# An attention and feed-forward kernel on one core: its opening replanned with a shared-port rule, paired scores and prescaled queries, and written in fixed order until chunk 3's x is turned

## The chip, the cores and the metric

The kernel runs on one core of one Trainium2 chip. The metric is device time in microseconds (us) of one execution, and the time of a kernel is the median of its runs. The engines are named as in the profile: PE is TensorE's matmul stream (PEld its weight loads), DVE is VectorE, ACT is ScalarE, POOL is GpSimd, SP is SyncE, which here only issues DMA transfers. "L1388" is line 1388 of the kernel.

## The reference

`q`, `k` and `v` have the shape batch 8, heads 8, sequence 576, head width 64. Two attentions are added: a coarse one over means of four tokens, and a local one over tokens less than four apart. The sum, laid out as 4608 tokens of width 512, is normalised and goes through a gated feed-forward layer with 1536 inner columns.

```python
q_d = q.reshape(B, H, Sd, 4, D).mean(axis=3)          # k_d, v_d likewise; Sd = 144
out_up = np.repeat(sm_attn(q_d, k_d, v_d), 4, axis=2)  # softmax attention, scale 1/8
mask = np.abs(pos[:, None] - pos[None, :]) < 4
scores = np.where(mask, scale * q @ k.T, -1e9)         # then softmax, then @ v
attn_out = out_up + out_local
x = attn_out.transpose(0, 2, 1, 3).reshape(B * S, H * D)
xn = x / np.sqrt(np.mean(x * x, -1) + 1e-6) * rms_g
g = xn @ w_gate
out = (g / (1 + np.exp(-g)) * (xn @ w_val)) @ w_out
```

## The kernel before

The tokens are worked through in 18 chunks of 256. A chunk has two stages. The first makes its `x`, normalises it and turns it, so that the 512 columns lie on partitions. The second (`Forward`) is the feed-forward layer: for each of six pairs n of 128-column blocks, `first` computes gate and value products into `ps_h` (L1388), ACT and DVE make the gated product from them (`tanh`, `gate` L1399, `product` L1404, `high` L1410, `low` L1413), and `second` multiplies it with the output weights into `ps_o` (L1427). Every f32 operand is split into a high and a low part and three products are added, so a pair takes 48 + 12 matmuls, and all 18 chunks take 5184 of L1388 and 1296 of L1427. Once chunks overlap, the feed-forward of one chunk runs on PE while DVE, ACT and POOL make the `x` of a later one.

There are two ways to make `x`. Chunks 2 to 17 use `Attention`: products of q and windows of k and v on DVE (L917, L921, L970, L980), with help from ACT and POOL. The first two chunks use `Early`, which is shorter and goes through PE. For each of a chunk's two units and each of four head pairs n, `score` puts a mask matmul (L1166, against `near_sb`) and the q times k matmuls (L1168) into a `ps_h` tile. DVE's `peak` finds the row maximum (L1181), `less` scales it (L1185), ACT's `powers` takes exponentials (L1192), DVE's `invert` makes the reciprocal of the sum (L1198, L1199), `edges` and `shares` multiply by it (L1211, L1219), PE turns the result (L1227, L1238), a copy brings it back to SBUF (L703 on ACT, L705 on DVE), and `value` (L1258) and `spread` (L1265) give a unit's rows in PSUM. `spread` adds the coarse attention of batch 0. Copy, squares, `rms`, three Newton steps (`root`, L729 to L731), `norm`, the turn of x (L1303) and its split into `xh` and `xl` (L1306, L1310) follow, and then the chunk's first L1388 can run.

The coarse attention (`Coarse`, per batch and head pair) is scores L593, maximum L603, its scaling L608, exponentials L613, reciprocal L644 and L647, turn L623, copies, values L638 and scaling L656. For batch 0 its sums over four tokens are made from loaded raw data, which `Early` also reads (L473 for q and k, L481 for v). For the other batches they are summed by DMAs that add.

All weights are decoded in the opening. They lie in HBM as 64-bit words; a piece is fetched by SP (L309), ACT scales it (L315), POOL extracts three last bits (L325), DVE joins them (L332), ACT makes the high part (L339, for gate and value multiplied by `g_sb`, the norm's gain) and DVE the low part (L346, L344).

The order of all this up to chunk 2's feed-forward and chunk 3's `x` is set by a planner in the kernel (`Plan`). A task has an engine (or a choice of two), a cost, a due time, predecessors and buffers. The planner goes forward in its own time: of an engine's ready tasks that could start within `NEAR` of the earliest, the one with the lowest number in the table `RANK` is next; DMA transfers are put one after another at `MB` us per MB. Within `tc.manual_schedule()` instructions are emitted in this order, until planned time `due[FIRST] + 10` (224 us); the rest of the planned tasks, and chunks 3 to 17 that follow in loops, are ordered by the framework's scheduler. An engine works its queue strictly in order.

Where the planner sees PE idle, `heat` (L504) puts in 512-column (or 256-column) bf16 matmuls into an unused tile, so that PE keeps its clock. Until the first `value` of `Early` that needs it, one of the two `ps_o` tiles is spare and takes them.

POOL's queue holds small loads (`load_edges` L1147, queries L906, `load_small` L1532 to L1536 with `min_sb`, `g_sb` and `same_sb`), `make_one` (`one_sb`, L1500), parts of L1151, L481, L970 and L1413, all of L325, and the adding DMAs (L417).

Of the kernel before, what the change touches and what calls it, by code (L numbers as in the profile page):

```python
# [1654 lines left out]
```

## Time and profile before

| | |
|---|---|
| median of 3 runs | 1091.54 us (1090.29 to 1092.67) |
| the profiled execution | 1089.94 us, of it 1088.1 us span of instructions |
| PE busy | 1066.7 us (98%), 7983 matmuls |
| DVE busy | 909.6 us (84%) |
| ACT busy | 598.6 us (55%) |
| POOL busy | 160.8 us (15%) |
| granted PE clock, mean | 0.992 |

The page gives busy times per engine, and the span in 40 slices of 27 us with a digit in tenths for each engine. A view of windows gives the same for chosen stretches, with the granted clock; a timeline lists instructions with their start and duration, and in brackets how long the engine stood idle before, and what ended that. A view of groups adds up the instructions of one line and shape: the count, total busy time, mean in ns of one, and idle time of the engine just before them. Busy PE includes `heat`, and a matmul's duration overlaps the next, so PE's share is not useful work.

### The profile page before, as it was taken

What the parts mean: (1) busy time and instruction counts of PE and PEld (TensorE: products, weight loads), DVE (VectorE), ACT (ScalarE), POOL (GpSimd) and SP (SyncE); (2) the same over time, 40 slices, a digit from 0 to 9 for tenths busy, and PEclk for the clock granted to TensorE, in tenths of its full rate; (3) what the DMA queues carried; (4) which work ended last, traced back from release to release, by engine and by line L of the source; (5) the groups of instructions that cost most, each with busy time, mean ns of one, the idle gap of its engine ahead of it and who ended that gap; (6) DMA issues with size and microseconds to landing.
All of it is one profiled execution on the core that took longest, in us unless ns stands there. A gap on an engine that the chain in (4) does not pass through costs nothing.

```text
span 1088.1 us, 21642 instructions
## 1 busy us (share of the span) xinstructions
PE 1066.7 (98%) x7983; PEld 970.2 (89%) x7983; DVE 909.6 (84%) x1554; ACT 598.6 (55%) x2029; POOL 160.8 (15%) x200
## 2 busy tenths in 40 slices
PE   7899999999999999999999999999999999999997
PEld 4569899899989999999999999999999999999996
DVE  7799999798969897979797979798998898986421
ACT  4686565737266565656564737383737373645111
POOL 6544564300210101010101010100000000000000
PEclk9899999999999999999999999999999999999999
DMA  9885657333654535353525253522221222210000
GB/s 292 274 237 167 182 134 155 77 91 86 132 102 117 118 99 102 107 106 87 126 85 128 68 130 86 132 77 82 63 86 54 79 78 74 80 40 20 1 20 20
DMA packets 79182, 114.09 MB, mean 105 GB/s; under 512 B 33038, under 2 KB 40406, under 8 KB 79076
## 3 DMA queue, kind: packets, MB, share of 16 engines
q1 hardware_dynamic: 48308, 88.40, 26.3%
q0 software_dynamic: 11680, 19.78, 11.6%
q10 hardware_dynamic: 19088, 4.53, 1.9%
q8 instruction: 62, 1.02, 0.4%
q14 instruction: 44, 0.36, 0.1%
HBM read 100.86 MB, written 11.80 MB: 104 GB/s over the span
## 4 chain that ended last, share of the span: by engine, by line
PE 85%; DVE 6%; DMA 3%; issue 2%; POOL 2%; ACT 1%; SPq 1%; DVEq 0%; POOLq 0%; ACTq 0%
PE ps_h L1388 51%; PE ps_o L1427 25%; PE ps_a L638 3%; DMA w<-in_w_val_dram 1%; PE ps_a L593 1%; PE ps_a L623 1%; DVE prod L917 1%; PE ps_a L1033 1%; DVE x_t L980 1%; DVE sc L921 1%; PE ps_a L1258 1%; DVE sil L1404 0%; POOL hs L1413 0%; DMA vs<-in_v_sum_dram 0%; DMA wo<-in_w_val_dram 0%
## 5 line engine op out<-in xcount | busy, mean ns | idle before, releaser
L1388 PE MATMUL ps_h<-xh,w 128*128 128x256 f32 x3456 | 632.6, 281 | 0.0
L1388 PEld LDWEIGHTS ps_h<-xh,w 128*128 128x128 f32 x3456 | 537.6, 188 | 9.7 <-issue 3.1
L1388 PE MATMUL ps_h<-xl,w 128*128 128x256 f32 x1728 | 482.5, 280 | 0.0
L1427 PE MATMUL ps_o<-wo,hs 128*128 128x512 f32 x1296 | 327.1, 396 | 4.2 <-POOL hs L1413 1.7
L1388 PEld LDWEIGHTS ps_h<-xl,w 128*128 128x128 f32 x1728 | 325.2, 188 | 5.8 <-issue 2.0
L963 ACT ACTIVATE prod<-kv,sc 128x64 f32<-128x64 f32 x1024 | 261.9, 406 | 28.9 <-DVE sc L954 15.5
L1427 PEld LDWEIGHTS ps_o<-wo,hs 128*128 128x128 f32 x1296 | 232.8, 188 | 49.1 <-DVE hs L1413 2.8
L980 DVE TENSOR_REDUCE x_t<-prod 128x128 f32<-128x896 f32 x128 | 134.5, 1080 | 39.5 <-PE ps_a L1033 36.8
L1410 ACT ACTIVATE hs<-sil 128x512 fp32r<-128x512 f32 x108 | 68.2, 631 | 165.5 <-DVE sil L1404 140.1
L1396 ACT ACTIVATE sil<-ps_h 128x512 f32<-128x512 f32 x108 | 64.1, 595 | 148.7 <-PE ps_h L1388 140.8
L917 DVE TENSOR_TENSOR prod<-q_t,kv 128x896 f32<-128x896 f32 x128 | 138.6, 1089 | 0.2
L921 DVE TENSOR_REDUCE sc<-prod 128x14 f32<-128x896 f32 x128 | 136.9, 1075 | 0.2
L1399 DVE SCALAR_TENSOR_TENSOR sil<-sil,ps_h 128x512 f32<-128x512 f32 x108 | 73.7, 683 | 52.1 <-ACT sil L1396 52.1
L970 DVE TENSOR_TENSOR prod<-sc,kv 128x384 f32<-128x384 f32 (+1 forms) x128 | 105.9, 868 | 0.1
L1404 DVE SCALAR_TENSOR_TENSOR sil<-sil,ps_h 128x512 f32<-128x512 f32 x108 | 73.9, 684 | 22.6 <-PE ps_h L1388 22.1
L417 POOL DMA_DIRECT2D qk<-in_qk_sum_dram x42 | 39.0, 928 | 340.0 <-DMA qk<-in_qk_sum_dram 282.1
L1413 DVE TENSOR_TENSOR hs<-sil,hs 128x512 fp32r<-128x512 f32 x102 | 69.9, 685 | 17.9 <-ACT hs L1410 17.8
L613 ACT ACTIVATE a_g<-ps_a,m_g 72x144 f32<-72x144 f32 x128 | 46.5, 370 | 54.2 <-DVE m_g L608 50.0
L417 POOL DMA_DIRECT2D vs<-in_v_sum_dram x42 | 39.4, 937 | 104.1 <-DMA vs<-in_v_sum_dram 80.7
L1003 ACT ACTIVATE up_t<-x_t 128x128 f32<-128x128 f32 x128 | 39.1, 305 | 18.3 <-DVE x_t L993 12.2
L638 PEld LDWEIGHTS ps_a<-vs,a_g 72*72 72x72 f32 x512 | 39.2, 150 | 7.4 <-ACT a_g L613 2.9
L638 PE MATMUL ps_a<-vs,a_g 72*72 72x64 f32 x512 | 40.8, 234 | 5.1 <-ACT a_g L613 2.7
(154 smaller groups left out, 808.0 us busy)
## 6 DMA issues: line engine op xcount, KB each, us to landing
kv<-in_k_pad_dram SPq DMA_DIRECT2D x56, 320.0 KB
kv<-in_v_pad_dram SPq DMA_DIRECT2D x56, 320.0 KB
qk<-in_qk_sum_dram POOLq DMA_DIRECT2D x42, 288.0 KB, 4.5
out_dram<-o_sb SPq DMA_DIRECT2D x96, 72.0 KB
vs<-in_v_sum_dram POOLq DMA_DIRECT2D x42, 144.0 KB, 4.3
q_t<-in_q_band_dram SPq DMA_DIRECT2D x150, 36.0 KB
w<-in_w_gate_dram SPq DMA_DIRECT2D x8, 512.0 KB
w<-in_w_val_dram SPq DMA_DIRECT2D x8, 512.0 KB
```

The costliest lines, as they stand in the source:

```text
L417: nc.gpsimd.dma_start(out=t, in_=(qk_sum, v_sum)[i][self.b, j, :, self.half], accum_op=ALU.add)
L638: nc.tensor.matmul(out=op[:, par, c], lhsT=at[:, kc, c * HALF:(c + 1) * HALF], rhs=self.sums.vs[:, 2 * (self.hp % 2) + par, kc], start=(kc ...
L917: nc.vector.tensor_tensor(out=pr, in0=bcast(q[:, s0:s0 + 2], 2, NO), in1=window(k, s0), op=ALU.mult)
L921: nc.vector.tensor_reduce(out=self.sc[:, j, par, s0:s0 + 2], in_=self.pr[i], axis=AX.X, op=ALU.add,)
L963: nc.scalar.activation(out=self.pr[i][:, o, s], in_=self.v[j, par][:, s0 + s + o], func=AF.Copy, scale=p[:, s, o:o + 1],)
L970: (nc.vector if engine == "DVE" else nc.gpsimd).tensor_tensor(out=self.pr[i][:, a:b], in0=bcast(p[:, :, a:b].rearrange("p s o -> p o s"), ...
L980: nc.vector.tensor_reduce(out=self.x[j][:, s0:s0 + 2, par], in_=pr.rearrange("p o s d -> p s d o"), axis=AX.X, op=ALU.add,)
L1388: self.last = nc.tensor.matmul(out=p[n][:, i], lhsT=wi[:, k], rhs=xi[:, k], start=(m == 0), stop=(m == 3 * KT - 1),).ins
L1399: nc.vector.scalar_tensor_tensor(out=self.sil[n], in0=self.sil[n], scalar=1.0, in1=self.g[n], op0=ALU.add, op1=ALU.mult,)
L1404: nc.vector.scalar_tensor_tensor(out=self.sil[n], in0=self.sil[n], scalar=0.5, in1=self.v[n], op0=ALU.mult, op1=ALU.mult,)
L1413: (nc.gpsimd if engine == "POOL" else nc.vector).tensor_tensor(out=self.hs[n][:, 1], in0=self.sil[n], in1=self.hs[n][:, 0], op=ALU.subtract,)
L1427: nc.tensor.matmul(out=self.o[j], lhsT=lhs[:, cols], rhs=rhs, start=(f == 0 and m == 0), stop=(f == NF - 1 and m == 2),)
```

## The change

- The planner's rules: a task that reads two tensors in SBUF on DVE (`port=True`), and every POOL task but a software DMA, does not start while a task of the other engine of that kind runs (`PORT`, `held`). PE costs count twice, and fill-ins half, before planned time 11.5 (`COLD`). `NEAR`, `WARM_AT`, `MB` and single costs are new.
- `RANK` is new (881 numbers for 879): all tasks of the opening are put in another order.
- `score` for one head pair becomes `scores` for two: two mask matmuls, then the q times k matmuls of the two pairs in turn, which lie on different 64 rows.
- The queries are copied with the factor -1/8 (`order`), and `one_sb` has the opposite sign; the scores come out negative and scaled, DVE takes a minimum, and `less` is gone. Exponentials use scale -1.
- In the planned tasks of `Coarse` and `Early`, the scaling of the maximum and the addition of 1e-9 move from DVE to ACT (`scale`, `more`), and `invert` is the reciprocal alone. In chunks that the loops emit they stay on DVE.
- `last_bits` may go to ACT, by the planner's choice; two do.
- `g_sb` is loaded by ACT right after `ident_sb`, no longer by POOL in `load_small`. `peak` of `Attention` names `load_small` as predecessor.
- The spare tile of `heat` is `ps_o0` alone, open from the start until chunk 0's x is turned; `Early`'s values use `ps_o1`.
- The fixed order ends when chunk 3's x has been turned, not at a planned time.

```diff
-NEAR = 0.15
-WARM_AT = 6.5
+NEAR = 0.05
+WARM_AT = 5.5
+COLD = 11.5
+PORT = {"DVE": "POOL", "POOL": "DVE"}
-MB = 3.1
+MB = 2.7
...
 RANK = [
-    -393, 85, 50, 17, 62, 1150, -215, -246, 10, -244, -122, -279, -318, 11, -155, 19, 355, 210, 148, 337, -1236,
...
+    -1640, 95, -479, -157, -190, -129, 116, 73, 242, 38, 314, 440, 6, -1675, -1703, 151, -47, -177, -105, -247,
...
+        t.port = ({"DVE"} if port else set()) | (set() if sw else {"POOL"})
...
-    def run(self, until=1e9):
+    def run(self, last=()):
...
+                        s = max(free[e], t.at, at, floor)
+                        if e in t.port:
+                            a, b = self.held[PORT[e]]
+                            s = b if a <= s < b else s
...
-            cost = next(o for o in t.options if o[0] == e)[1]
+            cost = next(o for o in t.options if o[0] == e)[1] * (2 if e == "PE" and s < COLD else 1)
...
-            nc.scalar.copy(out=self.q, in_=raw)
+            nc.scalar.activation(out=self.q, in_=raw, func=AF.Copy, scale=-0.125)
...
+                more = task("ACT", 0.2, lambda: self.more("ACT"), at, exps, uses=[z])
+            inv = task("DVE", 0.2, self.invert, at, [more], uses=[z])
...
-                    scored[n] = task("DVE", 0.42, lambda u=u, n=n: self.peak(u, n), at, [score], uses=[sps[n]])
-                powers = []
-                for half in range(2):
-                    less = task("DVE", 0.17, lambda u=u, h=half: self.less(u, h), at, [scored[2 * half], scored[2 * half + 1]])
...
+        def scores(self, u, half):
...
+            for n in pair:
+                nc.tensor.matmul(
+                    out=self.s[u, n], lhsT=one_sb, rhs=bcast(near_sb[:, FAC * (1 - lo):FAC * (1 - lo + NEAR_K)], 1, 2),
+                    start=True, stop=False,
+                )
             for h in range(2):
+                for par, n in enumerate(pair):
+                    rows = slice(par * D, (par + 1) * D)
+                    nc.tensor.matmul(
+                        out=self.s[u, n][:, h].rearrange("p (n j) -> p j n", j=FAC), lhsT=q[rows, h, FAC * n0:FAC * (n0 + GRP)],
+                        rhs=k[rows, h, :, n0 - lo:n0 - lo + NEAR_K], start=False, stop=(h == 1),
+                    )
...
-        bits = task("POOL", (0.75, 1.55)[m - 1], lambda: last_bits("POOL"), at, [got], uses=[raw])
+        bits = task(
+            (("POOL", (0.68, 1.13)[m - 1], at), ("ACT", (0.6, 1.03)[m - 1], at + 12)), 0, last_bits, at, [got], uses=[raw],
+        )
...
     nc.scalar.dma_start(out=ident_sb, in_=ident)
+    nc.scalar.dma_start(out=g_sb, in_=rms_g)
...
     plan.start()
     with tc.manual_schedule():
-        plan.run(due[FIRST] + 10)
+        plan.run(atts[FIRST].turned)
     plan.run()
```

The order shows the change on SP, whose queue brings what the opening reads. `w_1_` are places that hold the raw q and k sums and later a unit's values, `w_0_` the raw v sums, `w_2_` weight pieces. Before, the queue began so:

```order
L456 DMA w_1_100<-in_qk_sum_dram 128x4x576
L456 DMA w_1_102<-in_qk_sum_dram 128x4x576
L309 DMA w_2_128<-in_w_gate_dram 128x1024
L309 DMA w_2_128<-in_w_val_dram 128x1024
L462 DMA w_0_137<-in_v_sum_dram 72x4x512
L309 DMA w_2_128<-in_w_gate_dram 128x1024
L309 DMA w_2_128<-in_w_val_dram 128x1024
L462 DMA w_0_137<-in_v_sum_dram 72x4x512
L1134 DMA wo_1_120<-in_v_pad_dram 128x8x64
```

Now it begins so:

```order
L465 DMA w_1_102<-in_qk_sum_dram 128x4x576
L465 DMA w_1_104<-in_qk_sum_dram 128x4x576
L1156 DMA w_1_102<-in_v_pad_dram 128x8x64
L471 DMA w_0_130<-in_v_sum_dram 72x4x512 x2
L1156 DMA w_1_104<-in_v_pad_dram 128x8x64
L1156 DMA wo_1_127<-in_v_pad_dram 128x8x64
L318 DMA w_2_186<-in_w_gate_dram 128x1024
L318 DMA w_2_186<-in_w_val_dram 128x1024
L1156 DMA wo_1_210<-in_v_pad_dram 128x8x64
L318 DMA w_2_186<-in_w_gate_dram 128x1024
L318 DMA w_2_186<-in_w_val_dram 128x1024
```

Both v sums and three units' values stand ahead of the first weight pair, and the fourth unit's ahead of the second.

On ACT, the place is the first high part of a weight (`w_0_` from `w_2_` and `g_sb`) and what stands around it: exponentials of the coarse attention (`a_g,z_g`) and of `Early` (`w_1_`), and the copies of turned tiles (`prod`, `a_g`). Before:

```order
L613 ACTIVATE a_g,z_g<-ps_a,m_g 72x144 x2
L315 ACTIVATE w_2_238<-w_2_238 128x1024
L339 ACTIVATE w_0_359<-w_2_128,g_sb 128x8x128
L613 ACTIVATE a_g,z_g<-ps_a,m_g 72x144 x2
L1192 ACTIVATE w_1_102,z_e<-ps_h,m_e 128x136 x2
```

Now:

```order
L727 COPY prod<-ps_a 128x512
L683 DMA up<-xl_357 72x4x64
L324 ACTIVATE w_2_274<-w_2_274 128x1024
L348 ACTIVATE w_0_398<-w_2_186,g_sb 128x8x128
L727 COPY prod<-ps_a 128x512
L348 ACTIVATE w_0_398<-w_2_186,g_sb 128x8x128
L625 ACTIVATE m_g<-m_g 72x4
```

The first high part has moved behind the exponentials of the first two coarse head pairs, and a scale of the third weight pair and this high part now stand ahead of the second `prod` copy, which chunk 0's first `value` needs.

On POOL, the small loads stand against the weights' last bits (`w_2_`). Before:

```order
L325 TENSOR_SCALAR w_2_128<-w_2_128 128x1024
L481 TENSOR_TENSOR vs<-w_0_137 72x512
L1151 TENSOR_TENSOR kv<-kv,side_sb 64x512
L481 TENSOR_TENSOR vs<-vs,w_0_137 72x512
L1532 MEMSET min_sb 128x84
L1534 DMA min_sb<-in_band_min_dram 4x28 x4
L1535 DMA g_sb<-in_rms_g_dram 128x4
L1536 DMA same_sb<-in_same_tok_dram 128x128
L325 TENSOR_SCALAR w_2_238<-w_2_238 128x1024 x2
```

Now:

```order
L490 TENSOR_TENSOR vs<-w_0_130 72x512
L1173 TENSOR_TENSOR kv<-kv,side_sb 64x512
L490 TENSOR_TENSOR vs<-vs,w_0_130 72x512 x2
L1554 MEMSET min_sb 128x84
L1556 DMA min_sb<-in_band_min_dram 4x28 x4
L1557 DMA same_sb<-in_same_tok_dram 128x128
L334 TENSOR_SCALAR w_2_186<-w_2_186 128x1024 x2
L334 TENSOR_SCALAR w_2_274<-w_2_274 128x1024
```

The load of `g_sb` has left POOL's queue, and all last bits now come after the small loads.

More of the change, by code (lines that the diff above doesn't have):

```diff
@@ L136, in buf, with add @@
         return Buf(res)
-    def add(self, engine, cost, fn, due, after=(), with_=(), allocs=(), uses=(), not_before=0.0, dma=0.0, lag=0.0, hw=0, sw=0):
+    def add(self, engine, cost, fn, due, after=(), with_=(), allocs=(), uses=(), not_before=0.0, dma=0.0, lag=0.0, hw=0, sw=0, port=False):
         options = [(engine, cost, due)] if isinstance(engine, str) else list(engine)
@@ L168, in start @@
         ready = self.ready = {e: [] for e in free}
+        self.held = {e: (0.0, 0.0) for e in PORT}
         for t in self.tasks:
@@ L182, in open @@
             self.ready[e].append(t)
-    def run(self, until=1e9):
+    def run(self, last=()):
         free, ready = self.free, self.ready
-        while self.left:
+        while self.left and not (last and all(t.start is not None for t in last)):
             best = None
@@ L492, in heat @@
         if spare["open"] and made:
-            if "tile" not in spare:
-                spare["tile"] = ps_o.tile([P, DM], FP32, name="ps_o")
             out, fresh, n = spare["tile"], True, plan.gap
-        n, plan.idle, plan.gap = n * WARM_SHARE, 0.0, 0.0
+        n, plan.idle, plan.gap = n * plan.share, 0.0, 0.0
         cols = 1
@@ L531, in high @@
             def high():
+                self.more()
                 self.invert()
@@ L558, in plan @@
             ]
-            scale = task("DVE", 0.16, self.scale, at, peaks, uses=[m])
+            scale = task("ACT", 0.2, lambda: self.scale("ACT"), at, peaks, uses=[m])
             exps, copies = [], []
@@ L605, in attn_moe_kernel, with scale @@
         SC = 1.0 / (FAC * FAC * 8.0)
-        def scale(self):
-            nc.vector.tensor_scalar(out=self.m, in0=self.m, scalar1=-self.SC, scalar2=None, op0=ALU.mult)
+        def scale(self, engine="DVE"):
+            if engine == "ACT":
+                nc.scalar.activation(out=self.m, in_=self.m, func=AF.Copy, scale=-self.SC)
+            else:
+                nc.vector.tensor_scalar(out=self.m, in0=self.m, scalar1=-self.SC, scalar2=None, op0=ALU.mult)
         def powers(self, par):
@@ L641, in values, with more @@
                         )
+        def more(self, engine="DVE"):
+            if engine == "ACT":
+                nc.scalar.activation(out=self.z, in_=self.z, func=AF.Copy, scale=float(FAC), bias=FAC * 1e-9)
+            else:
+                nc.vector.tensor_scalar(
+                    out=self.z, in0=self.z, scalar1=1e-9, scalar2=float(FAC), op0=ALU.add, op1=ALU.mult,
+                )
         def invert(self):
-            nc.vector.tensor_scalar(
-                out=self.z, in0=self.z, scalar1=1e-9, scalar2=float(FAC), op0=ALU.add, op1=ALU.mult,
-            )
             nc.vector.reciprocal(out=self.z, in_=self.z)
@@ L1082, in plan @@
-                inv = task("DVE", 0.33, lambda u=u: self.invert(u), at, powers)
+                    for n in pair:
+                        scored[n] = task("DVE", 0.42, lambda u=u, n=n: self.peak(u, n), at, [score], uses=[sps[n]])
+                powers = [
+                    task("ACT", 0.62, lambda u=u, n=n: self.powers(u, n), at, [scored[n]], uses=[sps[n]]) for n in range(4)
+                ]
+                more = task("ACT", 0.2, lambda u=u: self.more(u), at, powers)
+                inv = task("DVE", 0.2, lambda u=u: self.invert(u), at, [more])
@@ L1180, in peak @@
                 self.z[u] = band.tile([P, H], FP32, name="z_e", bufs=4)
-            nc.vector.tensor_reduce(out=self.heads(self.m[u], n), in_=self.s[u, n], axis=AX.X, op=ALU.max)
-        def less(self, u, half):
-            m = self.m[u][:, half * KT:(half + 1) * KT]
-            nc.vector.tensor_scalar(out=m, in0=m, scalar1=-0.125, scalar2=None, op0=ALU.mult)
+            nc.vector.tensor_reduce(out=self.heads(self.m[u], n), in_=self.s[u, n], axis=AX.X, op=ALU.min)
         def powers(self, u, n):
@@ L1342, in plan @@
             att, c, T = self.att, self.c, due[self.c]
-            o_bufs = [buf("ps_o") for _ in range(2)]
+            o_bufs = [buf(f"ps_o{j}") for j in range(2)]
             last = None
@@ L1365, in plan @@
                 low = task(
-                    (("DVE", 0.6, soon), ("POOL", 1.55, soon)), 0, lambda e, n=n: self.low(n, e), soon, [high], uses=[sil, hs],
+                    (("DVE", 0.6, soon), ("POOL", 1.3, soon)), 0, lambda e, n=n: self.low(n, e), soon, [high], uses=[sil, hs], port=True,
                 )
@@ L1419, in second @@
             if f == 0:
-                self.o = [ps_o.tile([P, DM], FP32, name="ps_o") for _ in range(2)]
+                self.o = [ps_o.tile([P, DM], FP32, name=f"ps_o{j}") for j in range(2)]
             heat(self.o[0], fresh=f == 0)
@@ L1545, in attn_moe_kernel @@
     atts = [
-        Early(0).plan(X_DUE[0], (ps_h, "ps_h"), (ps_o, "ps_o")),
+        Early(0).plan(X_DUE[0], (ps_h, "ps_h"), (ps_o, "ps_o1")),
         Early(1).plan(X_DUE[1], (ps_h, "ps_h"), (ps_a, "ps_a")),
```

131 lines of the change are left out of this document (62 added, 69 removed), and 92 rows, old and new, of the table RANK.

## The prediction

> **What bounds the kernel now.** I read the page first, then a table of windows by stage, then timelines of the stages in which PE is not full.
>
> ```profile
> span 1088.1 us, 21642 instructions
> PE 1066.7 (98%) x7983; PEld 970.2 (89%) x7983; DVE 909.6 (84%) x1554; ACT 598.6 (55%) x2029; POOL 160.8 (15%) x200
> ```
>
> The windows give the stretch, its length, busy time of PE, PEld, DVE, ACT and POOL with instructions in brackets, the granted PE clock, the DMA share and GB/s.
>
> ```profile
> 0.00:78.20 78.20, 67.65 (x385) 42.57 (x386) 62.73 (x122) 52.09 (x140) 41.98 (x52) 0.91 0.88 276
> 78.20:200.00 121.80, 119.24 (x917) 107.91 (x916) 114.66 (x189) 76.13 (x216) 61.75 (x73) 1.00 0.62 149
> 250.00:350.00 100.00, 98.02 (x780) 89.07 (x779) 87.65 (x152) 60.18 (x236) 12.92 (x16) 1.00 0.49 114
> 400.00:500.00 100.00, 100.00 (x774) 92.95 (x773) 87.98 (x157) 57.40 (x208) 10.32 (x12) 1.00 0.43 104
> ```
>
> ```profile
> 78.22 0.47 PE L1388 MATMUL ps_h<-xh,w 128*128 128x256 f32 x1
> ```
>
> The feed-forward starts at 78.22 us. From 400 on PE is busy without a gap, and the change leaves that part's computation as it is. So the kernel is bound by PE behind an opening in which PE cannot yet do its main work, and the change can only move three things: the start of the feed-forward (A), what PE loses between 78 and 250 us (B), and what it loses between 250 and 350 (C). Until 78.2 PE's 67.65 us are mostly small products and fill-ins; DVE is the fullest engine that does nothing but needed work, 62.73 of 78.20, and again 114.66 of 121.80 after it. Its idle 15.5 us of the opening are the place to look.
>
> **A, the stall that goes.** One wait is named by both diff and trace: that for `g_sb`.
>
> ```profile
> 31.52 0.58 POOL L1535 DMA_DIRECT2D g_sb<-in_rms_g_dram  x1
> ```
>
> ```profile
> DMA to landing us min/median/max: 4.8/4.8/4.8
> ```
>
> ```profile
> 36.38 1.21 ACT L339 ACTIVATE w<-w,g_sb 128x1024 fp32r<-128x1024 f32 x1 [6.01 <-POOL w L325]
> ```
>
> ```profile
> 37.62 1.28 DVE L346 SCALAR_TENSOR_TENSOR w<-w,g_sb,w 128x1024 fp32r<-128x1024 f32 x1 [3.20 <-ACT w L339]
> 39.76 0.17 DVE L644 TENSOR_SCALAR z_g<-z_g 72x4 f32<-72x4 f32 x1 [0.86 <-ACT a_g L613]
> ```
>
> ```profile
> 38.36 1.22 PE L638 MATMUL ps_a<-vs,a_g 72*72 72x64 f32 x8 [2.71 <-ACT a_g L613]
> 40.53 1.22 PE L638 MATMUL ps_a<-vs,a_g 72*72 72x64 f32 x8 [0.95 <-DVE a_g L705]
> ```
>
> ```profile
> 35.00:40.00 5.00, 1.88 (x12) 1.47 (x12) 1.49 (x3) 3.62 (x16) 3.57 (x4) 0.74 0.67 185
> 40.00:45.00 5.00, 4.47 (x26) 3.84 (x27) 4.96 (x9) 4.35 (x8) 1.03 (x1) 0.50 0.65 224
> ```
>
> `g_sb`'s load is issued at 31.52 and lands 4.8 us later, at 36.3; ACT, in order, stands at L339 for 6.01 us until 36.38. The row blames POOL's L325, but the landing is what ends at that time. Behind L339 are the exponentials L613 and L1192, so DVE stands 3.20 and 0.86 us and PE 2.71 and 0.95, and PE's granted clock falls to 0.74 and then 0.50. The change loads `g_sb` at the start of ACT's queue, so this wait goes: DVE, the nearly full engine, gets back 3.20 + 0.86 = **4.06 us**. For PE's half clock I count nothing by itself: in the window after the wait DVE is 4.96 of 5.00 us busy, so it is not held up by PE there.
>
> **A, DVE's work ahead of the first product.** Groups of instructions of the first 78.2 us (count, busy us, mean ns of one, idle before):
>
> ```profile
> L1185 DVE TENSOR_SCALAR m_e<-m_e 128x4 f32<-128x4 f32 x8 | 3.5, 443 | 0.2
> L1198 DVE TENSOR_SCALAR z_e<-z_e 128x8 f32<-128x8 f32 x3 | 1.6, 526 | 0.7 <-ACT w L1192 0.7
> L608 DVE TENSOR_SCALAR m_g<-m_g 72x4 f32<-72x4 f32 x4 | 1.4, 354 | 0.1
> L644 DVE TENSOR_SCALAR z_g<-z_g 72x4 f32<-72x4 f32 x4 | 0.6, 159 | 0.9 <-ACT a_g L613 0.9
> L332 DVE SCALAR_TENSOR_TENSOR wo<-wo 128x1024 uint32<-128x1024 uint32 x4 | 4.9, 1221 | 0.0
> L705 DVE COPY prod<-ps_a 128x512 f32<-128x512 f32 x1 | 0.7, 656 | 0.0
> L481 DVE TENSOR_TENSOR vs<-vs,w 72x512 f32<-72x512 f32 x3 | 2.8, 943 | 0.1
> L1151 DVE TENSOR_TENSOR kv<-kv,side_sb 64x512 f32<-64x512 f32 x2 | 2.2, 1120 | 0.0
> ```
>
> The first four rows are what leaves DVE: 19 instructions, 3.5 + 1.6 + 1.4 + 0.6 = 7.1 us by their rows, but L644's 159 ns for as little data suggests that much of the other three is waiting inside the instruction, so at least 19 × 0.16 = 3.0. The order puts other work in ahead of the first product: one more join of 1024 columns (1.22), one of 512 (0.61 by half of it), one more L1151 (1.12), two copies of a unit's values out of PSUM (2 × 0.66), less one L481 (0.94) and one copy of `prod` (0.66); small copies, edges and a reciprocal add some 0.4. That is +3.1. The net lies between 3.1 − 7.1 = −4.0 and 3.1 − 3.0 = +0.1; I take **−1.5**, nearer to the end that L644's row gives, since its instruction is of the same kind.
>
> ACT takes up 12 of these small operations, the 8 in `Coarse` and 4 in `Early`. At L644's 0.16 us that is about 2 us; ACT has 52.09 of 78.20 busy, so I price it at 0 for the end, and at 2 if they stand in the chain one after another.
>
> **A, the new waits.** SP puts both v sums and three units' values ahead of the first weight pair, where the pair had stood behind the q and k sums alone.
>
> ```profile
> w<-in_w_val_dram SPq DMA_DIRECT2D x8, 512.0 KB
> w<-in_v_sum_dram SPq DMA_DIRECT2D x2, 576.0 KB
> w<-in_v_pad_dram SPq DMA_DIRECT2D x2, 256.0 KB
> ```
>
> ```profile
> 13.36 1.24 POOL L325 TENSOR_SCALAR w<-w 128x1024 uint32<-128x1024 uint16 x1 [2.18 <-DMA w<-in_w_val_dram]
> 19.86 1.48 POOL L325 TENSOR_SCALAR w<-w 128x1024 uint32<-128x1024 uint16 x1 [2.98 <-DMA w<-in_w_val_dram]
> ```
>
> ```profile
> 10.00:20.00 10.00, 10.00 (x49) 5.12 (x47) 6.67 (x15) 6.10 (x20) 4.79 (x9) 1.00 1.01 286
> 24.00:36.00 12.00, 11.57 (x59) 5.86 (x57) 9.98 (x20) 4.62 (x18) 9.30 (x13) 0.87 1.04 382
> ```
>
> That is 2 × 576 + 3 × 256 = 1920 KB or 1.97 MB more; at the 286 GB/s of 10 to 20 us the first pair lands 6.9 us later, at 13.36 + 6.9 = 20.2. The second loses one v sum and gains a fourth unit's values, so 1.64 MB, 5.7 us: 25.6. A third pair is 1.05 MB behind it, 2.8 us at the 382 GB/s of 24 to 36: 28.4. All last bits come after the small loads on POOL, that is from about 32 us if POOL keeps its times, where two had been done by 21. What is queued behind: joins on DVE, and on ACT the first high part, which stands ahead of copies and exponentials. DVE has other work there (9.98 of 12.00 busy from 24 to 36), so most is covered. Without cover the cost is at most the 6 us that ACT stood at L339 before, at least 0; I take **+2**.
>
> So A = −4.06 − 1.5 + 2 = **−3.6**, between −4.06 − 4.0 + 0 = −8.1 and −4.06 + 0.1 + 6 = +2.0.
>
> `one_sb` is made later, behind four query loads, and PE's fill-ins with it.
>
> ```profile
> 4.58 3.17 PE L504 MATMUL ps_o<-zero_sb,one_sb 128*128 128x512 bf16 x7 [4.58 <-POOL one_sb L1500]
> 12.42 4.02 PE L504 MATMUL ps_o<-zero_sb,one_sb 128*128 128x512 bf16 x9
> 18.22 1.69 PE L504 MATMUL ps_o<-zero_sb,one_sb 128*128 128x512 bf16 x7
> ```
>
> Each query load costs POOL about as much as `g_sb`'s 0.58, four 2.3 us. A fill-in takes 3.17/7 = 0.45 us at 4.58, 4.02/9 = 0.45 at 12.42 and 1.69/7 = 0.24 at 18.22, so PE is at half pace for the first 16 us or so. By the rows the two or three us shift that with no cost, as PE then waits for sums that are not there. The Trainium skill, page "TensorE: Matmul & The Clock Gate", section "What's actually happening", says that the clock is throttled by default and released after one busy window of about 3.4 us; by that rule PE would be at pace by 8 us before and about 10.5 now, and PE would not be the late one in the first 20 us at all. Here the trace disagrees, with half pace still at 12.42 us; if the rule held, A would be about 2 us better.
>
> **B, 78 to 250 us.** The fill-ins and waits of this stage, and the group of the second products:
>
> ```profile
> 115.75 1.26 PE L504 MATMUL ps_a<-zero_sb,one_sb 128*72 128x256 bf16 x10
> 123.15 1.47 PE L504 MATMUL ps_h<-zero_sb,one_sb 128*128 128x512 bf16 x6
> ```
>
> ```profile
> L1427 PE MATMUL ps_o<-wo,hs 128*128 128x512 f32 x309 | 81.1, 400 | 4.2 <-POOL hs L1413 1.7 <-DVE hs L1413 1.5 <-ACT hs L1410 0.8
> ```
>
> Of 78 to 350 us; and the part of it from 250 on:
>
> ```profile
> PE ps_o L1427 <- DVE hs L1413: 0.8, 1, 0.8
> PE ps_o L1427 <- ACT hs L1410: 0.8, 1, 0.8
> ```
>
> Fill-ins stand in an in-order queue, so the 1.26 + 1.47 = 2.7 us delay all behind them, where PE would not have waited anyway. The new order has none here. Of the waits 4.2 − 1.6 = 2.6 lie before 250. At most 2.7 + 2.6 = 5.3 us go. But DVE is 94% busy from 78 to 200, and PE waits there for what DVE makes; where DVE is no earlier, a missing fill-in becomes a wait. I take somewhat over half, **−3.3**, between −5.3 and +1 (a new wait of the size of the 0.8 rows).
>
> **C, 250 to 350 us.** The order has 27 fill-ins of 256 columns in chunk 3's feed-forward; before there were 5 at about 282. 22 × 0.126 (1.26/10) = +2.8, of which the waits of 0.8 and 0.8 may be what they replace: **+0.9**, between −1.6 and +3.
>
> Paired scores: the same number of matmuls in another sequence, in a stretch where PE has fill-ins; 0. Tail and chunks from 4 on: 0.
>
> **Sum.** −3.6 − 3.3 + 0.9 = −6.0. The profiled execution took 1089.94, so 1083.9; it lies 1.6 under the median 1091.54, so **1085.5** on the median's basis.
>
> **The rivals.**
>
> *The whole opening tightens* (0.15). The order then removes more than the named wait: DVE's 15.5 us idle fall further, A reaches its end of −8.1, B its −5.3, C 0: −13.4, or 1078. For it: DVE's idle before 78 is four times the wait that I count. Against: much of it lies ahead of the first data. The clock rule of the Trainium skill above would push this way.
>
> *The stall is replaced* (0.19). Weight bits that start at 32 us instead of 13, and ACT's and DVE's queues behind them, cost what `g_sb` cost: A = 0, B = −1, C = +0.9: about 1091.5, no change. For it: ACT's first high part still needs two joins that are late now. Against: DVE's queue holds coarse scalings ahead of them.
>
> *Slower by ACT's queue* (0.12). A scale of the third weight pair stands ahead of the `prod` copy that chunk 0's first value needs.
>
> ```profile
> 45.18 0.58 ACT L703 COPY prod<-ps_a 128x512 f32<-128x512 f32 x1
> ```
>
> That copy was at 45.18, and would be at about 41.5 by A. If the third pair lands later than about 40, each us later moves the first product, and from about 46 the kernel is slower; at 50, A = +5 or so, and with B at −1.5 and C at +0.9 the time is 1096. Against: it lands at 28.4 by the rates above, and 11 us are between. For: the DMA share is already 1.01 to 1.04 in these windows, so whatever is added queues.
>
> **How the numbers follow.** Forecast 0.54 (1080 to 1089), the tighter opening 0.15, no change 0.19, slower 0.12. About 0.2%, 2.2 us, can be told from no change: 1089.4 to 1093.7. Faster by more: the forecast, the tighter opening, and a third of "replaced": 0.54 + 0.15 + 0.06 = 0.75. Within: 0.12. Slower: the last case's 0.12 and a little of "replaced": 0.13. The range 1075.5 to 1093 leaves out most of the slower case and the tail of the tighter one.
>
> **What would show it.** Right: ACT's first L348 (formerly L339) without a wait of us behind `g_sb`; first L1407 (formerly L1388) at 72 to 77 us; no half clock near 40; PE's waits of 78 to 250 under 3 us; L518 (formerly L504) near 2.8 us in chunk 3's feed-forward. Wrong: the first L1407 at or after 78, then A failed; as early as 70, then DVE's idle was the larger term; PE waits for `hs` or weights `w` of more than 5 us between 78 and 250, then B did; ACT idle for several us at a third L324, then its queue did.

## The result, and the profile after

The changed kernel takes 1098.15 us, the median of 13 runs (1093.49 to 1104.73), and the kernel before 1091.30 (1089.48 to 1093.67, 13 runs). The ratio is 1.0060, with a 95% interval of 1.0047 to 1.0074: slower, where the forecast was 6 us faster. The profiled execution took 1095.07 us, 5.1 more than that of before.

The page's span and busy times:

```profile
span 1093.3 us, 21632 instructions
PE 1060.6 (97%) x7996; PEld 965.8 (88%) x7996; DVE 897.3 (82%) x1517; ACT 602.5 (55%) x2058; POOL 161.7 (15%) x199
```

DVE has 12 us less to do, PE is busy 6 us less, and the span is 5 us longer. The windows, cut at the places of before, say where:

```profile
0.00:75.64 75.64, 61.80 (x397) 38.01 (x397) 58.34 (x110) 57.61 (x157) 46.07 (x50) 0.93 0.84 279
75.64:200.00 124.36, 123.44 (x950) 112.38 (x949) 106.16 (x156) 70.64 (x206) 57.04 (x80) 1.00 0.61 145
240.00:250.00 10.00, 3.56 (x21) 2.63 (x19) 10.00 (x20) 0.00 (x0) 0.00 (x0) 0.79 0.42 116
250.00:350.00 100.00, 94.59 (x761) 86.62 (x761) 85.50 (x150) 61.76 (x243) 12.88 (x15) 0.97 0.48 108
40.00:45.00 5.00, 5.00 (x41) 4.19 (x41) 2.27 (x8) 4.89 (x19) 3.04 (x4) 0.56 0.92 343
```

The opening is shorter by 2.6 us, and PE loses less up to 200. But from 240 to 250 PE is busy for only 3.56 us, and from 250 to 350 it is idle for 5.4 us, where it had been idle for 2. From 40 to 45 PE is near half clock, as it was before. The next two rows are the first feed-forward product, and the first high part on ACT, which no longer waits:

```profile
75.64 0.47 PE L1407 MATMUL ps_h<-xh,w 128*128 128x256 f32 x1
```

```profile
35.44 1.23 ACT L348 ACTIVATE w<-w,g_sb 128x1024 fp32r<-128x1024 f32 x1
```

PE's timeline from 240 on follows, first after and then before. It shows the last second products that PE can do ahead of its wait (241.92), the turn of chunk 3's x (252.99, before 251.57) and that of chunk 4's (324.17, before 319.36):

```profile
241.92 1.64 PE L1446 MATMUL ps_o<-wo,hs 128*128 128x512 f32 x6
252.99 1.12 PE L1057 MATMUL ps_a<-ident_sb,x_t 128*128 128x128 f32 x4 [9.43 <-DVE x_t L1044]
...
324.17 1.04 PE L1057 MATMUL ps_a<-ident_sb,x_t 128*128 128x128 f32 x8
```

```profile
247.96 1.28 DVE L1020 TENSOR_TENSOR x_t<-x_t,rinv 128x512 f32<-128x512 f32 x2
251.57 1.04 PE L1033 MATMUL ps_a<-ident_sb,x_t 128*128 128x128 f32 x8
...
319.36 1.04 PE L1033 MATMUL ps_a<-ident_sb,x_t 128*128 128x128 f32 x8
```

PE comes to chunk 3's turn at 243.56 (252.99 less 9.43), 8.0 us sooner than before and with the same matmuls done, and waits 9.43 us. Before, the norm (L1020) ended at 249.24, and PE came to the turn 2.3 us after that, so no wait was to be seen. The turn is 1.4 us later than before, and chunk 4's turn 4.8 us. DVE's timeline shows what it did meanwhile:

```profile
239.91 0.16 DVE L742 TENSOR_SCALAR rms<-ps_a 128x8 f32<-128x8 f32 x1
239.98 1.07 DVE L945 TENSOR_REDUCE sc<-prod 128x14 f32<-128x896 f32 x1
240.97 1.08 DVE L941 TENSOR_TENSOR prod<-q_t,kv 128x896 f32<-128x896 f32 x1
241.97 0.16 DVE L745 TENSOR_SCALAR rinv<-rms 128x8 uint32<-128x8 uint32 x1
...
249.38 0.15 DVE L755 SCALAR_TENSOR_TENSOR rinv<-newton,rinv 128x8 f32<-128x8 f32 x1
...
251.65 1.28 DVE L1044 TENSOR_TENSOR x_t<-x_t,rinv 128x512 f32<-128x512 f32 x2
```

From `rms` to `norm` (L1044) chunk 3's root takes 11.7 us, since between its steps of 0.16 us stand chunk 4's products (L941) and sums (L945) of 1.08. Before, it took 9.3 (238.63 to 247.96): the planner had given the Newton steps to POOL, and gives them to DVE now. The fixed order fixes only the planner's own instructions among themselves; the framework's scheduler put chunk 4's between them. And chunk 3's x was late already. Its last addition on DVE, after and then before, is 5.0 us later, although the opening is 2.6 us shorter:

```profile
231.52 0.69 DVE L1017 TENSOR_TENSOR x_t<-x_t,up_t 128x512 f32<-128x512 f32 x1
```

```profile
226.53 0.68 DVE L993 TENSOR_TENSOR x_t<-x_t,up_t 128x512 f32<-128x512 f32 x1
```

DVE's busy time in two stretches, after and then before:

```profile
126.00:190.00 64.00, 64.00 (x513) 59.68 (x512) 50.10 (x80) 35.34 (x128) 29.80 (x46) 1.00 0.54 117
190.00:240.00 50.00, 49.94 (x369) 46.39 (x368) 36.69 (x56) 29.98 (x111) 11.63 (x14) 1.00 0.32 81
```

```profile
126.00:190.00 64.00, 63.95 (x525) 59.64 (x524) 60.85 (x110) 38.73 (x141) 31.01 (x38) 1.00 0.62 139
190.00:240.00 50.00, 48.64 (x352) 45.27 (x351) 41.42 (x61) 28.83 (x100) 9.83 (x12) 1.00 0.34 83
```

DVE idles 13.9 + 13.3 = 27.2 us now, and 3.15 + 8.58 = 11.7 before. These are three rows of its view of waits for 126 to 240 us now (total, times, longest):

```profile
DVE sil L1418 <- ACT sil L1415: 6.6, 4, 3.3
...
DVE z_g L671 <- ACT z_g L664: 3.4, 2, 1.9
...
DVE sil L1418 <- ACT z_g L664: 1.9, 1, 1.9
```

The first was 2.6 before; the others come with the moves of small operations to ACT.

### The profile page after: what moved, and what is told of

The parts are those of the page before. It is cut to its first block, busy times and chain, and to the rows that moved or that the text cites. A ratio compares the mean times of both kernels' runs of the same rounds, so it can differ in the third digit from the quotient of the medians.

```text
span 1093.3 us, 21632 instructions
## 1 busy us (share of the span) xinstructions
PE 1060.6 (97%) x7996; PEld 965.8 (88%) x7996; DVE 897.3 (82%) x1517; ACT 602.5 (55%) x2058; POOL 161.7 (15%) x199
## 4 chain that ended last, share of the span: by engine, by line
PE 83%; DVE 8%; DMA 3%; SPq 2%; ACT 2%; issue 2%; ACTq 0%; POOL 0%; DVEq 0%
PE ps_h L1407 50%; PE ps_o L1446 25%; PE ps_a L657 2%; DVE prod L941 2%; DVE sc L945 2%; PE ps_a L609 1%; DMA wo<-in_w_out_dram 1%; PE ps_a L1057 1%; ACT prod L987 1%; PE ps_a L642 1%; SPq L318 1%; DMA wo<-in_w_val_dram 1%; SPq L1156 1%; DVE x_t L1004 1%; PE ps_o L518 1%
## 5 line engine op out<-in xcount | busy, mean ns | idle before, releaser
L941 DVE TENSOR_TENSOR prod<-q_t,kv 128x896 f32<-128x896 f32 x128 | 140.5, 1103 | 0.2
L945 DVE TENSOR_REDUCE sc<-prod 128x14 f32<-128x896 f32 x128 | 137.5, 1080 | 0.0
L657 PE MATMUL ps_a<-vs,a_g 72*72 72x64 f32 x512 | 38.5, 228 | 0.0
```

The source lines that it names most:

```text
L657: nc.tensor.matmul(out=op[:, par, c], lhsT=at[:, kc, c * HALF:(c + 1) * HALF], rhs=self.sums.vs[:, 2 * (self.hp % 2) + par, kc], start=(kc ...
L941: nc.vector.tensor_tensor(out=pr, in0=bcast(q[:, s0:s0 + 2], 2, NO), in1=window(k, s0), op=ALU.mult)
L945: nc.vector.tensor_reduce(out=self.sc[:, j, par, s0:s0 + 2], in_=self.pr[i], axis=AX.X, op=ALU.add,)
```

## The experiments

A first theory (order) held that chunk 4's products ahead of chunk 3's norm are the cause; a second (DVE late in total), that x is late whatever stands where; a third, that the new end of the fixed order is. Each run's "before" is timed on its own chip; unless another run is named, the changed kernel's 1098.15 and 1.0060 are what a run is compared with. Edits are cut; "..." marks what is left out.

**The old end of the fixed order.**

```diff
...
-        plan.run(atts[FIRST].turned)
+        plan.run(due[FIRST] + 10)
```

> The changed kernel, but the fixed order ends at planned time 224 as before, not when chunk 3's x is turned. Theory 1 (order on DVE): PE stands 9.4 us before chunk 3's turn because chunk 4's 16 products and sums (17 us of DVE) stand in DVE's queue ahead of chunk 3's norm; DVE's order up to there is almost the same here, so the wait stays at 7 us or more and the time within 3 us of the changed kernel's 1098. Theory 2 (DVE late in total, by waits for ACT between 126 and 230): the same, within 3. Theory 3 (the ending rule): PE is no longer held in a fixed order and fills the wait with other work; the wait falls under 3 us and the time to 1088 to 1092.

1101.22 us, ratio 1.0101 (1.0071 to 1.0131). The third theory falls. The wait before a turn was 5.0 us in its profile.

**Chunk 3's root on POOL.**

```diff
-            root = task((("POOL", 4.3, T - 10), ("DVE", 1.65, T - 8)), 0, self.root, ...
+            root = task((("POOL", 4.3, T - 10), ("DVE", 1.65, T - 8))[:1 if c == FIRST else 2], 0, ...
```

> The changed kernel with chunk 3's three Newton steps on POOL, as before the change, instead of DVE, where each of the nine small steps stood behind a product of 1.08 us of chunk 4. Theory 1: the norm no longer comes behind the steps' turns in DVE's queue; 12 POOL operations took some 6 us before, against 11 us from rms to norm now, so the wait falls by 3 to 6 us and the time by 3 to 5. Theory 2: the later chunks stay late, so the time moves by less than 2. Theory 3: no change, less than 2.

1095.13, ratio 1.0035 (1.0020 to 1.0051): 3.0 us of the loss, as the first theory had it. The wait before the turn was 2.3 us.

**Chunk 4's DVE work behind chunk 3's norm.**

```diff
...
-                    todo.pop(0)[1]()
+                    with tc.issue_after(att.normed) if c == FIRST else nullcontext():
+                        todo.pop(0)[1]()
```

> The changed kernel with DVE's work of chunk 4 (and of the coarse pairs emitted with it) queued behind chunk 3's last norm. Theory 1: chunk 3's turn comes at about 244 instead of 253, PE's wait of 9.4 us falls under 2, its clock stays up, and the time falls by 8 to 10, to 1088 to 1090. Theory 2: chunk 4's x is then late by as much instead, PE waits between 290 and 330, and the time stays within 3 us. Theory 3: within 3 us.

1097.86, ratio 1.0065 (1.0044 to 1.0085): no gain. Chunk 3's turn came at 245.39, without a wait of PE's, and yet chunk 4's was as late as in the changed kernel:

```profile
245.39 0.60 PE L1057 MATMUL ps_a<-ident_sb,x_t 128*128 128x128 f32 x4
...
325.11 1.04 PE L1057 MATMUL ps_a<-ident_sb,x_t 128*128 128x128 f32 x8
```

PE waits after 300 us instead, for the gated product of chunk 3 and for the low part of chunk 4's x, among others:

```profile
PE ps_o L1446 <- ACT hs L1429: 3.4, 3, 1.8
PE ps_h L1407 <- DVE xl L1065: 2.3, 1, 2.3
```

So the wait of 9.4 us, the most striking row of the trace, can be taken away without a gain, because others take its place. The first theory falls for the order of chunk 4's work; the second stands, which expected PE to wait between 290 and 330. Between this profile's time (1097.56) and chunk 4's turn lie 772.5 us; in the changed kernel it is 1095.07 − 324.17 = 770.9, before 1089.94 − 319.36 = 770.6. So the changed kernel's loss lies ahead of chunk 4's turn.

**Small operations of batches 1 and 2 back on DVE.**

```diff
-            scale = task("ACT", 0.2, lambda: self.scale("ACT"), at, peaks, uses=[m])
+            scale = task("ACT", 0.2, lambda: self.scale("DVE" if b else "ACT"), at, peaks, uses=[m])
...
-            more = task("ACT", 0.2, lambda: self.more("ACT"), at, exps, uses=[z])
+            more = task("ACT", 0.2, lambda: self.more("DVE" if b else "ACT"), at, exps, uses=[z])
```

> The changed kernel with the scaling of the maximum and the addition of 1e-9 of the coarse attention of batches 1 and 2 back on DVE, in the same order (nine pairs or so between 126 and 230 us). Theory 1: DVE gains the waits of 3.4 and 1.9 us for z_g but also 16 to 18 small operations of 0.16, so chunk 3's x is earlier by 1 to 3 us and the time lower by 1 to 3. Theory 2: DVE's late total is what counts, so 3 to 5 us go. Theory 3: under 1 us.

1097.18, ratio 1.0061 (1.0040 to 1.0083): not told from the changed kernel.

Four runs on the kernel before, whose order they keep, then price the edits one by one.

**`g_sb` early, alone.**

```diff
     nc.scalar.dma_start(out=ident_sb, in_=ident)
+    nc.scalar.dma_start(out=g_sb, in_=rms_g)
...
-        nc.gpsimd.dma_start(out=g_sb, in_=rms_g)
...
```

> The kernel before, with only the load of g_sb moved from POOL's small loads to ACT's queue at the start; every engine's order is otherwise the same. The forecast's term for this was 4.06 us of DVE. Chain theory (chunk 4's x, made by DVE, sets the time: in six profiles the time is its turn on PE plus 770.6 to 772.5 us): the opening's gain reaches chunk 4 through DVE's queue, 2 to 4 us lower, 1087.5 to 1089.5. Rival (the feed-forward's steps in DVE's queue wait for PE anyway, or the half clock comes back elsewhere): under 1 us.

1090.75, ratio 0.9991 (0.9978 to 1.0004): no gain that can be told. ACT's stall at L339 is gone, but the exponentials ahead of it now come behind another one, at the issue of a store (L659), which by the profile a load's landing ended; PE waits 5.5 us for them, where its longest wait at the old stall was 2.71:

```profile
29.41 0.57 ACTq L659 DMA_DIRECT2D up<-xl  x1
30.03 0.38 ACT L613 ACTIVATE a_g<-ps_a,m_g 72x144 f32<-72x144 f32 x1 [5.91 <-DMA wo<-in_v_pad_dram]
```

```profile
PE ps_a L623 <- ACT a_g L613: 5.5, 1, 5.5
```

The half clock comes back too, at another place:

```profile
62.00:70.00 8.00, 7.45 (x24) 4.28 (x25) 7.69 (x19) 5.21 (x17) 3.63 (x3) 0.57 0.79 271
```

**The instruction edits in the old order**, with `g_sb` early: prescaled queries and no `less`, and the moves to ACT.

```diff
-            nc.scalar.copy(out=self.q, in_=raw)
+            nc.scalar.activation(out=self.q, in_=raw, func=AF.Copy, scale=-0.125)
...
-            nc.vector.tensor_scalar(out=m, in0=m, scalar1=-0.125, scalar2=None, op0=ALU.mult)
+            return
...
-            nc.vector.tensor_scalar(out=self.m, in0=self.m, scalar1=-self.SC, scalar2=None, op0=ALU.mult)
+                nc.scalar.activation(out=self.m, in_=self.m, func=AF.Copy, scale=-self.SC)
```

> The kernel before, in its old order, with the edits to single instructions: g_sb early, prescaled queries without the scaling of Early's maximum, and the scaling and the 1e-9 of the planned coarse and early attention on ACT. No paired scores, no new planner rules, no new table. Chain theory: the edits are good or neutral and the new order loses the time: 3 to 6 us lower than the kernel before, 1085 to 1088. Rival (the moves to ACT put waits into DVE's queue whatever the order): within 2 us of the kernel before, or slower.

1091.79, ratio 0.9998 (0.9979 to 1.0016).

**The same without the moves to ACT.**

> As the run with the edits in the old order, but without the moves to ACT: g_sb early and the eight scalings of Early's maximum left out. Chain theory: the run with g_sb early less 8 times 0.16 to 0.44 us, so 1 to 3.5 us lower than that, 1085 to 1088. Rival (the moves to ACT cost waits): this run is 2 us or more faster than the one with them; without that cost, 1 to 3 slower.

1087.27, ratio 0.9969 (0.9948 to 0.9989): this version beats both kernels, and the moves to ACT cost 1091.79 − 1087.27 = 4.5 us. The edit moves 28 operations, 12 of them in the opening, so this is the price of all 28. In the run with them DVE waits in the first 126 us for two operations that had been its own:

```profile
DVE z_g L653 <- ACT z_g L648: 7.4, 4, 4.7
DVE z_e L1204 <- ACT z_e L1203: 3.4, 4, 1.8
```

That is 10.8 us of waits for instructions that save DVE 0.16 us each; ACT, which stands in order behind exponentials and weights, comes to them late. From the first feed-forward product to chunk 3's last addition on DVE it is 152.5 us with the moves (227.98 − 75.47) and 148.5 without (225.07 − 76.54), one profile each. Leaving `less` out is worth 1090.75 − 1087.27 = 3.5 us.

**Four sums of chunk 3 twice, in the kernel before.**

```diff
-            nc.vector.tensor_reduce(
+            for _ in range(2 if self.c == FIRST and i < 4 else 1):
+                nc.vector.tensor_reduce(
...
```

> The kernel before, with the first four of chunk 3's eight score sums on DVE done twice (same result): 4 times 1.08 = 4.3 us more of DVE's work at 150 to 200 us, nothing else. Chain theory: chunk 4's turn and the time come 3 to 4.5 us later, 1094.5 to 1096. The forecast's picture (PE is the bound from 78 us on, DVE has room): 0 to 1 us.

1093.78, ratio 1.0029 (1.0019 to 1.0039): 4.3 us more for DVE cost 2.4, somewhat less than the chain theory's 3 to 4.5, and far more than the 0 to 1 of the forecast's picture. Chunk 4's turn moved by 2.7, and PE has two waits, at 150 to 155 us, that it did not have before:

```profile
322.06 1.04 PE L1034 MATMUL ps_a<-ident_sb,x_t 128*128 128x128 f32 x8
...
PE ps_a L623 <- ACT a_g L613: 1.2, 1, 1.2
PE ps_h L1389 <- DVE sil L1400: 1.1, 1, 1.1
```

So DVE has little to spare at that place, and its lateness reaches the end as waits of PE.

Four runs on the changed kernel.

**All small operations on DVE**: as above, for batch 0 and `Early` too.

> The changed kernel, in its order, with every move of small operations to ACT undone (scaling of the coarse maximum, the 1e-9 of coarse and early attention, the opening's too). In the old order these moves cost 4.5 us (1091.79 against 1087.27). If they cost the same in the new order (theory A: DVE stands behind ACT's queue for z_g and z_e), the time falls by 3 to 5, to 1093 to 1095. Theory B (the new order has placed them where DVE would wait for something else): less than 1.5.

1095.88, ratio 1.0045 (1.0025 to 1.0065): 2.3 us by the medians, between the two theories; the intervals overlap, so it is not told from the changed kernel.

**The fixed order only up to planned time 120.**

> The changed kernel with the fixed order ended at planned time 120; what the planner has left is ordered by the framework's scheduler. If the fixed order between 126 and 240 us is what leaves DVE idle for 27 us there (before 12), the scheduler fills some of it, chunk 4's turn comes at 316 to 322 and the time is 1088 to 1093. If the idle comes from what feeds DVE (buffers, PE's pace) and not from the order, or the scheduler orders no better, the time is 1096 or more.

1094.59, ratio 1.0041 (1.0020 to 1.0062): 3.6 us better by the medians, at the edge of what can be told, and chunk 4's turn at 322.06. Chunk 3's last addition comes 149.2 us after the first feed-forward product (223.53 − 74.38), where it is 155.9 in the changed kernel and 148.3 before. So the new table makes chunk 3's x late; but PE now waits at 160 to 210 us, and the kernel before stays ahead.

**All small operations on DVE, and the root on POOL.**

> The changed kernel with all small operations back on DVE and chunk 3's Newton steps on POOL. Theory A: the two gains add, 3 us of the root (measured 1095.13) and 3 to 5 of the small operations: 1090 to 1092.5. Theory B: the root's alone, 1094 to 1096.

1092.31, ratio 1.0004 (0.9985 to 1.0023): the loss against the kernel before is gone. This is 5.8 us under the changed kernel and 2.8 under the run with the root alone, so here the moves are told apart. Chunk 3's last addition still comes 156.0 us after the first feed-forward product (231.53 − 75.50): what is gained lies behind it.

**Half sums for chunk 3**, which leave out half of each sum.

```diff
-                out=self.sc[:, j, par, s0:s0 + 2], in_=self.pr[i], axis=AX.X, op=ALU.add,
+                out=self.sc[:, j, par, s0:s0 + 2], in_=self.pr[i][:, :, :, :D // 2] if self.c == FIRST else self.pr[i],
...
```

> The changed kernel in its order, with chunk 3's eight score sums over half of the 64 products each (half of the sum is left out): 8 times 0.54 = 4.3 us less of DVE's work at 185 to 200 us. Chain theory: chunk 4's turn and the time come 1.5 to 4.3 us earlier, as 4.3 us more cost 2.4 in the kernel before. Rival (DVE stands there for ACT and PE whatever it has to do): less than 1.

1099.88, ratio 1.0076 (1.0049 to 1.0102): nothing gained. The chain theory in its simple form, DVE's amount of work, falls in the new order. As the rival had it, DVE's waits there are no shorter (its largest, for ACT's `sil`, is 7.7 us, in the changed kernel 6.6), and the same wait of 9.4 us before chunk 3's turn appears again: the stretch from `rms` to `norm` takes as long here (243.98 to 255.73).

Three more runs for what was left.

**PE kept busy in its wait.** 36 fill-ins right before chunk 3's first turn.

```diff
+            for _ in range(36 if self.c == FIRST and j == 0 else 0):
+                nc.tensor.matmul(
+                    out=tp.rearrange("p a b -> p (a b)"), lhsT=one_sb, rhs=bcast(zero_sb, 1, 32), start=True, stop=True,
+                )
```

> The changed kernel with 36 more fill-ins of 512 columns (36 x 0.215 = 7.7 us) on PE right before chunk 3's first turn, in the 9.4 us in which PE stands there, so that its clock stays up; the framework's scheduler then orders some later instructions otherwise. Clock theory: the half clock from 246 to 256 us is what makes the stretch from the first feed-forward product to chunk 4's turn long (248.5 us, old order 241.1); it falls by 3 to 5 and so does the time. Chain theory (the turn waits for DVE's x, and chunk 4's x follows): within 1.5 of the changed kernel.

1100.70, ratio 1.0088 (1.0057 to 1.0119). The clock was full from 244 to 256, and no time was gained. But the half clock only came later, from about 264 to 271:

```profile
244.00:256.00 12.00, 10.33 (x49) 5.22 (x49) 11.90 (x30) 1.88 (x5) 0.00 (x0) 1.00 0.38 105
266.00:268.00 2.00, 2.00 (x9) 1.41 (x8) 1.97 (x4) 2.00 (x10) 0.00 (x0) 0.50 0.56 138
```

So the clock theory's gain did not come, but the run does not show what the half clock costs.

**The same with 12 fill-ins**, on the run that had lost its loss.

> The run with all small operations on DVE and the Newton steps on POOL (1092.31), with 12 fill-ins of 512 columns (2.6 us) before chunk 3's first turn. There PE waited 1.9, 0.5 and 0.6 us between 243 and 252 and was at half clock from 246 to 257. Clock theory: no half clock there, 2 to 5 lower, 1087.5 to 1090. Chain theory: within 1.5.

1096.50, ratio 1.0038 (1.0020 to 1.0055), 4.2 us slower than without them, which neither theory expected. Here too the half clock came later:

```profile
262.00:264.00 2.00, 2.00 (x10) 1.53 (x9) 2.00 (x4) 2.00 (x9) 0.00 (x0) 0.50 0.84 158
```

What a half-clock stretch costs stays open.

**That run without the late fill-ins.**

```diff
-        n = plan.idle
+        n = plan.idle if plan.free["PE"] < 200 else 0.0
```

> The run with all small operations on DVE and the Newton steps on POOL, without the fill-ins planned after 200 us (27 of 256 columns, in chunk 3's feed-forward; the forecast's term C, 2.8 us). If they stand in PE's path: 1.5 to 3.5 lower than 1092.31. If they only fill what PE would wait for DVE: within 1.

1090.55, ratio 0.9991 (0.9975 to 1.0007): 1.8 us by the medians, at the edge of what can be told.

Two instants order all of it, the first feed-forward product (F) and chunk 4's turn (T). The table has them from the profiles, with PE's idle time between them:

| run | time | F | T | T − F | PE idle, F to T | time − T |
|---|---|---|---|---|---|---|
| before | 1089.94 | 78.22 | 319.36 | 241.1 | 3.0 | 770.6 |
| `g_sb` early | 1090.97 | 78.84 | 320.43 | 241.6 | 3.4 | 770.5 |
| old order, no moves to ACT | 1088.62 | 76.54 | 317.93 | 241.4 | 3.0 | 770.7 |
| old order, all edits | 1089.74 | 75.47 | 319.09 | 243.6 | 5.3 | 770.7 |
| old order, 4.3 us more DVE | 1092.72 | 78.08 | 322.06 | 244.0 | 5.0 | 770.7 |
| changed | 1095.07 | 75.64 | 324.17 | 248.5 | 11.3 | 770.9 |
| chunk 4 behind | 1097.56 | 76.85 | 325.11 | 248.3 | 7.3 | 772.5 |
| small operations on DVE | 1095.88 | 73.60 | 324.94 | 251.3 | 12.0 | 770.9 |
| half sums | 1099.88 | 77.29 | 328.88 | 251.6 | 12.6 | 771.0 |
| root on POOL | 1095.99 | 78.96 | 324.90 | 245.9 | 5.6 | 771.1 |
| both | 1092.21 | 75.50 | 320.16 | 244.7 | 4.2 | 772.1 |
| both, no late fill-ins | 1090.73 | 74.22 | 316.16 | 241.9 | 7.2 | 774.6 |

Rows for two of them follow, the version that beats both kernels, and both repairs (small operations on DVE and the root on POOL):

```profile
76.54 0.47 PE L1387 MATMUL ps_h<-xh,w 128*128 128x256 f32 x1
...
317.93 1.04 PE L1033 MATMUL ps_a<-ident_sb,x_t 128*128 128x128 f32 x8
```

```profile
75.50 0.47 PE L1407 MATMUL ps_h<-xh,w 128*128 128x256 f32 x1
...
320.16 1.03 PE L1057 MATMUL ps_a<-ident_sb,x_t 128*128 128x128 f32 x8
```

In ten of these twelve the time after T is 770.5 to 772.1, whatever was done ahead of it; in the five runs that are not in the table it is 770.9 to 771.7. That says that the losses lie ahead of T; it does not make chunk 4's x the bound, since PE is nearly full behind T and a later event on PE would date the end as well. In the changed kernel's profile the opening F is 2.6 us shorter than before, but T − F is 7.4 us longer. PE's idle time makes most of that: PE's busy time between F and T is 237.2 to 240.9 us in eleven of the twelve (234.7 without the late fill-ins).

## Why the prediction was wrong

**The step that failed** is the one from PE's earlier arrival to the end, in terms B and C. B said that "where DVE is no earlier, a missing fill-in becomes a wait", and bounded such a wait at 1 us; C had no new wait; and no term asked when chunk 3's `x` would be ready. The runs show one wait of 9.43 us for it. The picture behind the terms, "the kernel is bound by PE behind an opening", holds as a sum. These are the stretches from F to T, before and then after:

```profile
78.22:319.36 241.14, 238.15 (x1834) 217.41 (x1833) 213.55 (x357) 139.04 (x448) 79.14 (x102) 1.00 0.52 125
75.64:324.17 248.53, 237.22 (x1837) 216.94 (x1836) 205.61 (x332) 137.39 (x459) 76.56 (x105) 0.98 0.52 125
```

F came 2.6 us sooner, PE was busy 0.9 less, it was idle 11.3 us instead of 3.0, and 0.3 came behind T: −2.6 − 0.9 + 8.3 + 0.3 = +5.1, the difference of the two profiles. What the picture hid is that PE had little to spare ahead of what DVE makes: x was ready only 2.3 us before PE's turn, and 4.3 us more for DVE cost 2.4. The forecast read that DVE was 94% busy up to 200, but not what DVE had to finish by 252. None of its signs of being wrong named x; two of its signs of being right, L348 without a wait and the first product at 72 to 77 us, came true in a slower kernel.

**A** had the right sign and nearly the size for the profiled execution (75.64 against 78.22, −2.6 for −3.6). That is in part luck: the profile is 3.1 us under the kernel's median, and seven runs with the same opening had F from 74.38 to 81.55. The reason was another one, too. The term of 4.06 us for `g_sb` measured 0.6 in the old order, inside the uncertainty: with the wait gone, the next one in ACT's queue took its place. DVE's removed operations were put at −1.5 in all; `less` alone was worth 3.5. Twelve operations on ACT were priced at 0, and at 2 at most. The change moves 28, 16 of them behind the opening, and together they cost 4.5 in the old order: the price is not the 0.16 us of one operation but the wait for ACT's queue.

**B** had the right sign for PE's arrival: PE came to chunk 3's turn 8.0 us sooner, of which 2.6 are F, so 5.4 were gained against 3.3 forecast. But none of it reached the end, since chunk 3's x was not sooner but later: its last addition by 5.0 us, and its root took 11.7 us for 9.3.

**C** was put at +0.9, with +3 as its worse end. From chunk 3's turn to chunk 4's it was 324.17 − 252.99 = 71.2 against 319.36 − 251.57 = 67.8, 3.4 more, behind a wait of 9.4 that the forecast did not have. The fill-ins were costed at 2.8 and measured 1.8, at the edge of what can be told. The root's change of engine (3.0 us) was in the order, and no step looked at it.

**The sum by runs**, in medians: `g_sb` −0.6, `less` −3.5, the moves to ACT +4.5, and 1098.15 − 1091.79 = +6.4 for the rest, that is new rules and table, paired scores and the new end of the order. Of that rest the root is 3.0 and the late fill-ins 1.8, measured in the new order. What remains, some 1.6 us, is not assigned: the paired scores and the loads' order were not tried by themselves. Each of these terms is uncertain by some 2 us, and the moves measured less in the new order (2.3 to 2.8) than in the old, so the sum is a rough one. What is shown is that undoing the moves and the root's change together takes the whole loss away. The version with both repairs and no late fill-ins is, by its ratio, still slower than the old order with two edits, though the intervals overlap, and its profile has 774.6 us behind T; why was not tried.

**The rivals.** The one on the slow side named ACT's queue at the third weight pair, ahead of a `prod` copy. ACT's queue has a part in the loss, by the moves, but not there: that copy ran at 36.56, where it had run at 45.18. "The stall is replaced" described well what `g_sb` alone did.

**The clock.** "No half clock near 40" was wrong, see 40 to 45. The Trainium skill, page "TensorE: Matmul & The Clock Gate", section "What's actually happening", puts the throttle after an idle window of about 3.4 us. In the wait of 9.43 us the trace agrees that the clock falls (0.79 from 240 to 250). But in the run with both repairs PE went to half clock between 246.4 and 246.8, after a wait of only 1.86 us and ahead of the next one, by its timeline and its windows:

```profile
245.93 0.44 PE L642 MATMUL ps_a<-ident_sb,a_g 72*72 72x72 f32 x4 [1.86 <-ACT a_g L727]
...
247.58 2.07 PE L1446 MATMUL ps_o<-wo,hs 128*128 128x512 f32 x4 [0.49 <-DVE hs L1432]
```

```profile
236.00:246.00 10.00, 8.14 (x53) 6.80 (x52) 10.00 (x16) 1.67 (x4) 1.17 (x6) 1.00 0.42 118
246.40:246.80 0.40, 0.40 (x2) 0.05 (x1) 0.40 (x1) 0.07 (x1) 0.40 (x1) 0.66 0.22 59
246.00:257.00 11.00, 9.95 (x54) 8.44 (x55) 9.40 (x19) 2.12 (x7) 3.79 (x7) 0.53 0.28 77
```

There the measurement decides: less than 3.4 us of idle time is enough here.

## What to carry to other kernels

Where a full engine is to arrive sooner, ask when its next input is ready: a gain ahead of that input becomes a wait for it. To place a loss, find an event whose distance to the end is the same in several runs, and split the time ahead of it into the full engine's work and its idle time. The longest wait in the trace can be removed without a gain, since a removed stall is worth only what the next waits leave of it. Moving a short operation to a less busy engine costs the wait in that engine's queue, not its duration.
